# Gated memory attention with an MLP, one core: a tile's outputs gathered through DRAM and summed on VectorE in place of selection matmuls

## The chip, the core and the metric

The kernel runs on one core of a Trainium2 chip. A core has TensorE (matrix multiplication), VectorE, ScalarE, GpSimd, and SyncE, which here only issues DMAs (SP in the profile). The metric is the device time of one execution in microseconds, as the median of several runs.

## The reference, cut to what matters

```python
h = jnp.concatenate([mem, xs], axis=1)          # 8 memory rows and 32 rows of x: one segment of 64
q, k, v = (einsum('btd,dhe->bhte', h, W) for W in (Wq, Wk, Wv))     # 32 heads of 128
scores = where(mask, einsum('bhqe,bhke->bhqk', q, k) * scale, -1e9)
o = einsum('bhqk,bhke->bhqe', softmax(scores), v)
o = einsum('bhte,hed->btd', o, Wo)              # 512 wide
mem = o[:, :8, :]                               # the memory of the next segment
outs.append(o[:, 8:, :])
...
a = concatenate(outs, axis=1)                   # 2048 rows
b = gelu(layernorm(x) @ w1 + b1) @ w2 + b2
out = g * a + (1 - g) * b                       # g = sigmoid(sum(x * gate_w)), one number per row
```

The segments are a recurrence: segment s + 1 needs the 8 memory rows that segment s gives.

## The kernel before, in words

The 2048 rows are 16 tiles (T) of 128 rows; a tile is four segments (si = 0 to 3) of 32 rows. First comes a stage that computes (1 - g) * b for all rows and puts it in DRAM (`c_dr`), while the attention weights are loaded. Then the loop of line 665 runs the 64 segments in order. The order of the instructions on every engine is the order of the program text (`manual_schedule`, line 292); each engine, and SP with its DMAs, takes its own in that order and waits where it must.

A projection or an output projection has 32 columns only, so four matmuls run side by side on four quarters of TensorE's array, each adding up a quarter of the reduction. Such a set of four matmuls of 512 columns is called a unit here. After it the four partial sums of a token lie in four groups of 32 partitions. A segment's main pass has room for 24 of its 32 rows beside the 8 of the memory (`RIDE` = 24); the other 8 rows of each of a tile's four segments (`LEFT` = 8) are collected and done once per tile as extra work, spread in the waits of the recurrence.

One segment of the loop, in the order of the text:

- `prep_h` (GpSimd, line 239) places the next segment's x columns; `x_norm(s-1)` (GpSimd, line 643) scales the previous segment's attention results by the reciprocals of its softmax sums, which come back over DRAM broadcast to all partitions (`Rb`). Its results go into `UT`, for this segment's output projection, and into `UL`.
- SP's loads: in si = 0 `c_load(T-2)` (line 205), `vp_load` (line 182) for the next segment, in si = 0 `load_xT(T+2)` (line 96), a transposing DMA.
- Projections (line 122) into the four banks `U`, each cast by ScalarE (line 127) and transposed by VectorE (line 131); scores; exponentials; the value projection (line 141).
- `run(W1)`: as many pieces of the extra work as W1 says, one unit each. `recip_x` (lines 627 to 635): VectorE's reciprocals, the DMA to `r_dr` (line 630) and back as `Rb` (line 631), the copies into `R`, a copy of the mask (line 252).
- `av`: attention times values (lines 283, 288), and ScalarE's copies into `UT` (line 746).
- `run(W2)`, then the output projection `wo_pass` (line 153) into bank `W`, cast by ScalarE in three cuts into `w` (line 650). `w` holds the four partial sums of the memory rows of this segment and of the other 24 rows of the segment before.
- `run(W3)`, then `out_sel` where there is one.
- `new_mem` in three parts (line 659), with one unit of extra work between them: small matmuls with `SelM` that add the four partial sums of the memory rows, and VectorE's casts into the next `hT` (line 661), from which the next segment's projections read.

The extra work of a tile is dealt out by `side(T, si)`: in si = 0, 1 and 3 projections of the next tile's left rows, eight units each; in si = 2 the output projection of the previous tile's left rows (`wo_left`), whose result `wl` ScalarE casts. Tile 15 has none in si = 0, 1, 3. The numbers of units are in

```python
WS = ((2, 3, 0), (2, 2, 2), (2, 2, 2), (2, 2, 2))
```

`out_sel(T-2)` (lines 221 to 235) is run in si = 0 from T = 2 on, and once for tile 14 behind the loop. It takes the four `w` and the `wl` of tile T - 2 and adds the four partial sums of every row in bank `U[2]`, by four matmuls with the 0/1 matrix `SelR` (line 223) and four with `SelL` (line 227). VectorE then multiplies by g and adds `c` (line 232), and SP stores 128 rows of the output (line 233). That piece is put in VectorE's list `dve_q`, which is emptied at the segment's end.

Of the kernel before, what the change touches and what calls it, by code (L numbers as in the profile page):

```python
# [9 lines left out]
FP32 = mybir.dt.float32  # L10
BF16 = mybir.dt.bfloat16
I32 = mybir.dt.int32
ACTF = mybir.ActivationFunctionType
ALU = mybir.AluOpType
# [13 lines left out]
def kernel(ctx, tc, A_x, A_mem0, A_Wq, A_Wk, A_Wv, A_Wo, A_seg_len, B_x, B_w1, B_b1, B_w2, B_b2, gate_w, out):  # L28
    nc = tc.nc
    P = 128  # L30
    _, S, Dm = A_x.shape
    H, Dh = A_Wq.shape[1], A_Wq.shape[2]
    M = A_mem0.shape[1]
    seg = int(A_seg_len)
# [4 lines left out]
    NT = S // P  # L39
    SPT = P // seg  # L40
# [6 lines left out]
    RIDE = 32 - M  # L47
# [6 lines left out]
    out2 = out.rearrange("b s d -> (b s) d")  # L54

    pers = ctx.enter_context(tc.tile_pool(name="pers", bufs=1))
    dram = ctx.enter_context(tc.tile_pool(name="dram", bufs=1, space=DRAM))
# [4 lines left out]
    ident = pers.tile([P, P], BF16)  # L62
    g_all = pers.tile([P, NT], FP32)
    c_dr = dram.tile([S, Dm], BF16, name="c_dr")
    r_dr = [dram.tile([P, NG], FP32, name=f"r_dr{i}") for i in range(2)]


# [26 lines left out]
    def load_xT(T):  # L94
        xT = ew.tile([P, KC, P], BF16, tag="xT", bufs=3, name="xT")
        nc.sync.dma_start_transpose(out=xT[:], in_=x2[T * P:(T + 1) * P, :])
        xTs[T] = xT
# [7 lines left out]
    U = [lps.tile([P, 512], FP32, name=f"U{i}") for i in range(4)]  # L105
# [55 lines left out]
    def flush(q, n=1):  # L161
        for _ in range(min(n, len(q))):
            q.pop(0)()
# [17 lines left out]
    def vp_load(T, si):  # L181
        nc.sync.dma_start(VP[T % 2][:, si].rearrange("p v e -> p (v e)"), VLs[T][si:P:SPT].rearrange("p a v e -> p a (v e)"))
# [18 lines left out]
    ws, wls, cs = {}, {}, {}  # L201

    def c_load(T):
        c = cw.tile([P, Dm], BF16, tag="c", name="c")
        nc.sync.dma_start(c[:], c_dr[T * P:(T + 1) * P, :])
        cs[T] = c
# [14 lines left out]
    def out_sel(T, bk):  # L221
        for si in range(SPT):
            nc.tensor.matmul(bk[32 * si:32 * si + 32, :], lhsT=SelR[:], rhs=ws.pop(SPT * T + si)[:], start=True, stop=False,
                             skip_group_check=True, tile_position=(0, 32 * si))
        wl = wls.pop(T)
        for si in range(SPT):
            nc.tensor.matmul(bk[32 * si:32 * si + 32, :], lhsT=SelL[:, 32 * si:32 * si + 32], rhs=wl[:], start=False, stop=True,
                             skip_group_check=True, tile_position=(0, 32 * si))

        def ev():  # L230
            o = cw.tile([P, Dm], BF16, tag="o", name="o")
            nc.vector.scalar_tensor_tensor(out=o[:], in0=bk[:], scalar=g_all[:, T:T + 1], in1=cs.pop(T)[:], op0=ALU.mult, op1=ALU.add)
            nc.sync.dma_start(out2[T * P:(T + 1) * P, :], o[:])
        dve_q.append(ev)
        yield

    def prep_h(s):
        T, si = divmod(s, SPT)
        nc.gpsimd.tensor_copy(out=hT[s % 3][:, :, 0:RIDE], in_=xTs[T][:, :, seg * si:seg * si + RIDE])
# [10 lines left out]
    def mask_put(i2):  # L250
        c = 4 * EW + (NG + 2 * M if i2 == 0 else 0)
        nc.vector.tensor_copy(out=(SbF, W)[i2][:, 0:c], in_=MkF[:, 0:c])
# [311 lines left out]
    cw = loop.enter_context(tc.tile_pool(name="cw", bufs=2))  # L564
# [17 lines left out]
    def run(n):  # L582
        for _ in range(n):
            next(fill, None)
# [5 lines left out]
    def side(T, si):  # L590
        gens = []
        if si == 2:
            if T >= 1:
                gens.append(wo_left(T - 1, X1))
        elif T + 1 < NT:
            gens = [[left_qk(T + 1, 0, 0, X1), left_qk(T + 1, 1, 0, X2)], [left_qk(T + 1, 0, 1, X1), left_qk(T + 1, 1, 1, X2)], [],
                    [left_v(T + 1, 0, X1), left_v(T + 1, 1, X2)]][si]
        return chain(*gens)

    def extra(T, si):  # L600

        if si == 0 and T >= 2:
            return out_sel(T - 2, U[2])
        return iter(())

    XRs, Rbs = {}, {}

    xs8 = SbF[:, 4 * EW:4 * EW + NG]
# [29 lines left out]
    def x_norm(s):  # L638
        T, si = divmod(s, SPT)
        XR, Rb = XRs.pop(s), Rbs.pop(s)[:].rearrange("p (c q) (h j) -> p h j c q", c=4, h=2)  # L640
        for out, o, a, b in ((UT[(s + 1) % 2], M, LEFT, 32), (UL[T % 2], LEFT * si, 0, LEFT)):
            for h in range(2):
                nc.gpsimd.tensor_tensor(out=out[:, :, 4 * h:4 * h + 4, o:o + b - a], in0=XR[:, :, 4 * h:4 * h + 4, a:b], in1=Rb[:, h, :, :, a:b], op=ALU.mult)  # L643
# [17 lines left out]
        nc.vector.tensor_copy(out=hn[:, k0:k0 + nk, RIDE:32], in_=bk.rearrange("p (k m) -> p k m", k=nk))  # L661


    WS = ((2, 3, 0), (2, 2, 2), (2, 2, 2), (2, 2, 2))
    for s in range(nseg):
        T, si = divmod(s, SPT)
        last = s == nseg - 1
        hc, hn = hT[s % 3], hT[(s + 1) % 3]
        W1, W2, W3 = WS[si]
        fill = side(T, si)  # L670
        if s + 1 < nseg:
            prep_h(s + 1)
        if s >= 1:
            x_norm(s - 1)
        if si == 0 and T >= 2:
            c_load(T - 2)
        if si < 3:
            vp_load(T, si + 1)
        if last:
            c_load(T - 1)  # L680
            c_load(T)
        if si == 0 and T + 2 < NT:
            load_xT(T + 2)
        for n, (t, hf) in enumerate(((0, 0), (1, 0), (0, 1), (1, 1))):
            bk = U[n]
            for kc in range(KC):
                qk_unit(bk, hc, t, hf, kc)
            if n == 0:
                flush(act_q, 9)
                flush(dve_q, 9)  # L690
            qk_tr(qk_cast(bk[:]), (QT, KT)[t], hf, LEFT * (1 - t))
            if n == 0:
                mask_put(1)
        V = cw.tile([P, NG, Dh], BF16, tag="V", name="V")
        E = cw.tile([P, NG, EW], BF16, tag="E", name="E")
        R = cw.tile([P, NG * 40], FP32, tag="R", name="R")
        Rs[s] = R
        xsum = SbF[:, 0:32 * NG].rearrange("p (i q) -> p i q", q=32)

        def exps(i2, x):  # L700
            c = slice(0, 40) if x else slice(40, EW)
            nc.scalar.activation(out=E[:, 4 * i2:4 * i2 + 4, c], in_=Sb[i2][:, :, c], func=ACTF.Exp, scale=scale)  # L702

        def msum(i2):
            sums(U[i2][:, 320:352].rearrange("p (i q) -> p i q", q=8), E[:, 4 * i2:4 * i2 + 4, :], 40, 48, 8, True)

        def mnorm(i2):
            r, e = RP[i2], E[:, 4 * i2:4 * i2 + 4, 40:56].rearrange("p i (a q) -> p i a q", q=8)
            nc.vector.reciprocal(out=r, in_=U[i2][:, 320:352])
            nc.vector.tensor_tensor(out=e, in0=e, in1=r.rearrange("p (i q) -> p i q", q=8).unsqueeze(2).to_broadcast([P, 4, 2, 8]), op=ALU.mult)  # L710

        scores(s, 0)
        nc.scalar.activation(out=E[:, 0:4, :], in_=Sb[0], func=ACTF.Exp, scale=scale)
        for kc in range(KC):
            v_unit(X1, hc, 0, kc)

        def v_cast(vb, h):
            i0 = 4 * vb + 2 * h
            nc.scalar.copy(out=V[:, i0:i0 + 2, :].rearrange("p i e -> p (i e)"), in_=(X1, X2)[vb][:, 256 * h:256 * h + 256])  # L719

        v_cast(0, 0)
        v_unit(X2, hc, 1, 0)
        if not last:
            xsums(E, 0)
            msum(0)
            mnorm(0)
        scores(s, 1)
        exps(1, 0)
        v_cast(0, 1)
        exps(1, 1)  # L730
        for kc in range(1, KC - 1):
            v_unit(X2, hc, 1, kc)
        if not last:
            msum(1)
            mnorm(1)
        v_unit(X2, hc, 1, KC - 1)
        for h in range(2):
            v_cast(1, h)
        if last:
            break  # L740
        run(W1)
        xsums(E, 1)
        recip_x(s)
        av(s, V, E)
        for j in (0, 2, 1, 3):
            nc.scalar.copy(out=UT[s % 2][:, j, :, 0:M], in_=U[j][:, 0:NG * 40].rearrange("p (i q) -> p i q", q=40)[:, :, 32:40])  # L746
        x_raw(s)
        run(W2)
        prep_q(s + 1)
        w = wo_pass(UT[s % 2], (0, P, 2 * P, Dm))  # L750
        if s >= 1:
            ws[s - 1] = w
        run(W3)
        for _ in extra(T, si):
            pass
        new_mem(w, hn, 0)
        run(1)
        new_mem(w, hn, 1)
        run(1)
        new_mem(w, hn, 2)  # L760
        for _ in fill:
            pass
        if si == 3 and T + 2 < NT:
            left_x(T + 2)
        flush(dve_q, 9)
        nc.vector.tensor_tensor(out=rmin[:, 0:RW], in0=rmin[:, 0:RW], in1=R[:, 0:RW], op=ALU.min)
        flush(act_q, 9)
# [33 lines left out]
    wl, c = wls.pop(T), cs.pop(T)  # L801
# [11 lines left out]
    o = cw.tile([P, Dm], BF16, tag="o", name="o")  # L813
# [128 lines left out]
```

## Time and profile before

| | |
|---|---|
| median of 3 runs | 770.96 us (770.31 to 771.15) |
| span of the profiled execution, first to last instruction | 768.4 us |
| mean granted TensorE clock in it | 0.996 |
| busy: TensorE, ScalarE, VectorE, GpSimd | 753.4, 540.0, 396.1, 278.2 us |
| 16 DMA engines, queue of SP | 26.8% of their time |

The profiled execution's time is known by its span; what lies around it (start and end of the program) is the 2.6 us to the median. Times in rows are microseconds from the span's start. A row of a merged view has start, length, engine, line, what is written and read, how many instructions; a bracket at its end tells how long the engine was idle before it and what ended that. In rows of groups the numbers behind the bar are the busy time in all, the mean of one in ns, and the idle time before them. PEld is TensorE's loading of weights, which lies beside its matmuls. Rows with SPq are SP's DMA issues: the length is that of the issue, not of the transfer.

### The profile page before, as it was taken

How to read it: one execution, taken by the hardware profiler on the slowest of the kernel's cores; microseconds unless marked ns; L12 is line 12 of the kernel's file. 1: busy time of each engine (PE TensorE's matmuls, PEld its weight loads, DVE VectorE, ACT ScalarE, POOL GpSimd, SP SyncE). 2: the span in 40 equal slices, each digit the busy share in tenths (PEclk: the TensorE clock that was granted, in tenths of full speed). 3: DMA queues.
4: the chain of work that ended last, by engine and by line, in shares of the span. 5: the costliest groups of instructions: out<-in, count | busy, mean ns of one | idle time of the engine just before them, and what ended most of it. 6: DMA issues, size and time to landing. Idle time of an engine off the chain costs nothing.

```text
span 768.4 us, 43822 instructions
## 1 busy us (share of the span) xinstructions
PE 753.4 (98%) x19186; PEld 412.2 (54%) x19186; DVE 396.1 (52%) x1428; ACT 540.0 (70%) x1631; POOL 278.2 (36%) x522
## 2 busy tenths in 40 slices
PE   7999999999999999999999999999999999999996
PEld 5666554555555555555555555555555555555553
DVE  5776355445445454545554554545454555444444
ACT  4666676777777777777777777777777777777763
POOL 4111033433344443334434334443424443343341
PEclk9999999999999999999999999999999999999999
DMA  6779422223222222212131322122222213122221
GB/s 196 274 233 400 153 58 63 76 63 87 65 59 66 79 72 73 80 53 74 58 89 62 90 63 79 45 80 73 80 72 59 76 49 89 62 83 64 72 67 38
DMA packets 53319, 70.58 MB, mean 92 GB/s; under 512 B 21306, under 2 KB 43043, under 8 KB 51587
## 3 DMA queue, kind: packets, MB, share of 16 engines
q1 hardware_dynamic: 51394, 64.84, 26.8%
q8 instruction: 152, 2.49, 1.4%
q0 software_dynamic: 784, 1.97, 0.8%
q10 hardware_dynamic: 944, 0.92, 0.3%
q14 instruction: 45, 0.36, 0.2%
HBM read 56.96 MB, written 4.45 MB: 80 GB/s over the span
## 4 chain that ended last, share of the span: by engine, by line
PE 96%; DMA 1%; DVE 1%; ACT 1%; issue 0%; SPq 0%; POOL 0%; DVEq 0%; ACTq 0%
PE U L122 30%; PE X L141 18%; PE W L153 15%; PE X L122 7%; PE U L468 4%; PE U L283 4%; PE X L153 4%; PE W L462 2%; PE SbF L462 2%; PE U L270 1%; PE W L259 1%; DMA w_sb<-in_B_w_dram 1%; PE U L659 1%; PE SbF L259 1%; PE SbF L616 1%; PE U L288 1%
## 5 line engine op out<-in xcount | busy, mean ns | idle before, releaser
L643 POOL TENSOR_TENSOR UT<-XR,Rb 128x384 bf16<-128x384 bf16 x126 | 140.3, 1136 | 301.7 <-DMA Rb<-r_dr 220.5
L127 ACT CAST Tb<-U 128x512 bf16<-128x512 f32 x258 | 151.2, 586 | 78.4 <-PE U L122 78.1
L122 PEld LDWEIGHTS <-hT 128*32 128x32 bf16 x4096 | 104.5, 96 | 103.9 <-DVE hT L661 8.6
L141 PE MATMUL X<-Wv_sb,hT 128*32 128x512 bf16 x2048 | 143.8, 378 | 0.0
L122 PE MATMUL U<-Wq_sb,hT 128*32 128x512 bf16 x2048 | 136.1, 381 | 0.3 <-DVE hT L661 0.2
L122 PE MATMUL U<-Wk_sb,hT 128*32 128x512 bf16 x2048 | 132.7, 379 | 0.0
L153 PE MATMUL W<-Wo_sb,UT 128*32 128x512 bf16 x2080 | 124.6, 380 | 1.2 <-POOL racc L635 1.2
L661 DVE CAST hT<-U 128x8 bf16<-128x8 f32 x126 | 20.9, 167 | 172.8 <-PE U L659 163.6
L719 ACT CAST V<-X 128x256 bf16<-128x256 f32 x256 | 88.7, 372 | 14.5 <-PE X L141 0.8
L131 DVE STREAM_TRANSPOSE QT<-Tb 128x256 f32<-128x256 f32 x128 | 57.0, 446 | 76.5 <-ACT Tb L127 76.5
L153 PEld LDWEIGHTS <-UT 128*32 128x32 bf16 x2080 | 57.8, 96 | 56.5 <-issue 13.1
L650 ACT CAST w<-W 128x128 bf16<-128x128 f32 (+1 forms) x192 | 46.0, 311 | 48.2 <-PE W L153 48.2
L622 ACT CAST XR<-U 128x256 bf16<-128x256 f32 x252 | 78.4, 434 | 0.0
L131 DVE STREAM_TRANSPOSE KT<-Tb 128x256 f32<-128x256 f32 x128 | 57.0, 445 | 28.0 <-ACT Tb L127 23.5
L643 POOL TENSOR_TENSOR UL<-XR,Rb 128x128 bf16<-128x128 bf16 x126 | 60.3, 502 | 0.0
L141 PEld LDWEIGHTS <-hT 128*32 128x32 bf16 x2048 | 46.4, 94 | 21.0
L635 POOL TENSOR_TENSOR racc<-racc,R 128x72 f32<-128x72 f32 x63 | 21.3, 338 | 93.4 <-PE U L288 84.1
L468 PE MATMUL U<-w_sb,hTm 128*128 128x512 bf16 (+1 forms) x176 | 52.4, 381 | 0.0
L746 ACT CAST UT<-U 128x64 bf16<-128x64 f32 x252 | 35.4, 226 | 22.9 <-PE U L288 22.8
L462 PEld LDWEIGHTS <-w_sb 128*128 128x128 bf16 (+1 forms) x352 | 34.5, 102 | 20.1 <-issue 1.3
L702 ACT ACTIVATE E<-W 128x64 bf16<-128x64 f32 (+1 forms) x128 | 35.0, 273 | 11.3 <-PE W L263 11.3
L659 PEld LDWEIGHTS <-w 128*32 128x32 bf16 x1008 | 22.8, 93 | 37.2 <-ACT w L650 29.3
(159 smaller groups left out, 1204.7 us busy)
## 6 DMA issues: line engine op xcount, KB each, us to landing
Rb<-r_dr SPq DMA_DIRECT2D x63, 512.0 KB, 3.8
Wv_sb<-in_A_Wv_dram SPq DMA_DIRECT2D x4, 1024.0 KB, 6.3
Wq_sb<-in_A_Wq_dram SPq DMA_DIRECT2D x4, 1024.0 KB, 7.1
Wk_sb<-in_A_Wk_dram SPq DMA_DIRECT2D x4, 1024.0 KB, 9.4
Wo_sb<-in_A_Wo_dram SPq DMA_DIRECT2D x4, 1024.0 KB, 15.0
VP<-VL SPq DMA_DIRECT2D x64, 64.0 KB, 3.5
c<-c_dr SPq DMA_DIRECT2D x16, 128.0 KB, 3.6
xt<-in_A_x_dram SPq DMA_DIRECT2D x15, 128.0 KB, 3.1
```

Of the source, the lines that this page charges most:

```text
L122: nc.tensor.matmul(bk[32 * j:32 * j + 32, :], lhsT=G[:, kc, :], rhs=W5[t][:, kc, h0:h1, j, :], start=(kc == 0), stop=(kc == KC - 1), tile_ ...
L127: nc.scalar.copy(out=Tb[:], in_=bk.rearrange("p (a b e) -> p a e b", a=8, b=2))
L131: nc.vector.transpose(out=dst[:, 8 * hf:8 * hf + 8, c0:c0 + 32, :].rearrange("p a r b -> p a (r b)").bitcast(FP32), in_=Tb[:].rearrange("p ...
L141: nc.tensor.matmul(bk[32 * j:32 * j + 32, :], lhsT=G[:, kc, :], rhs=Wv5[:, kc, 4 * vb:4 * vb + 4, j, :], start=(kc == 0), stop=(kc == KC - ...
L153: nc.tensor.matmul(bk[32 * c:32 * c + 32, :], lhsT=U_[:, j, i, :], rhs=Wo_sb[:, 4 * i + j, :], start=(n == 0), stop=(n == NW - 1), tile_po ...
L462: nc.tensor.matmul(hp[:rows, 0:TB * P], lhsT=w1_sb[:, kc, fc * P:fc * P + rows], rhs=yTs[blk][:, kc, :], start=(kc == 0), stop=(kc == KC - 1))
L468: nc.tensor.matmul(bp(blk, tt)[:], lhsT=hTm[blk % 2][:rows, fc, tt * P:(tt + 1) * P], rhs=w2_sb[:rows, fc, :], start=(fc == 0), stop=(fc = ...
L622: nc.scalar.copy(out=XR[:, j], in_=U[j][:, 0:NG * 40].rearrange("p (i q) -> p i q", q=40)[:, :, 0:32])
L643: nc.gpsimd.tensor_tensor(out=out[:, :, 4 * h:4 * h + 4, o:o + b - a], in0=XR[:, :, 4 * h:4 * h + 4, a:b], in1=Rb[:, h, :, :, a:b], op=ALU ...
L650: nc.scalar.copy(out=w[:, a:b], in_=W[:, a:b])
L719: nc.scalar.copy(out=V[:, i0:i0 + 2, :].rearrange("p i e -> p (i e)"), in_=(X1, X2)[vb][:, 256 * h:256 * h + 256])
L746: nc.scalar.copy(out=UT[s % 2][:, j, :, 0:M], in_=U[j][:, 0:NG * 40].rearrange("p (i q) -> p i q", q=40)[:, :, 32:40])
```

## The change

Outputs of tiles 0 to 13 no longer go through `out_sel` in the loop. Instead:

- `put_w`: each segment's `w` (128 x 512, four partial sums) is stored to DRAM at the top of the segment two later.
- `get_w`: two segments after that, the 24 rows are loaded back, so that the four partial sums of a token lie side by side in one partition of a tile `G` (128 x 4 x 512).
- `put_left`: `wl` of tile T - 1 is stored at the top of si = 3 of tile T; `get_left(T-2)`: at the top of si = 0 of tile T four DMAs load the 8 rows per segment of tile T - 2 from there into `G`.
- `add_parts(T-2)`: three additions and the multiply-add with g and `c` on VectorE, two of the four in si = 0 and two in si = 1 of tile T, placed behind `x_raw`; then the store of the output.
- W1, W2, W3 become 2, 2, 2 in every segment. `out_sel` stays for tile 14, behind the loop, and the last tile's own end is as it was.

All the new DMAs are issued by SP. The `w_dr` and `l_dr` buffers are double, by the parity of the tile.

```diff
+    w_dr = [dram.tile([SPT, P, Dm], BF16, name=f"w_dr{i}") for i in range(2)]
+    l_dr = [dram.tile([P, Dm], BF16, name=f"l_dr{i}") for i in range(2)]
...
+    def put_w(s, w):
+        T, si = divmod(s, SPT)
+        nc.sync.dma_start(w_dr[T % 2][si], w[:])
+
+    def put_left(T):
+        nc.sync.dma_start(l_dr[T % 2][:], wls.pop(T)[:])
+
+    def get_w(s):
+        T, si = divmod(s, SPT)
+        if si == 0:
+            Gs[T] = cw.tile([P, 4, Dm], BF16, tag="G", name="G")
+        nc.sync.dma_start(Gs[T][seg * si:seg * si + RIDE], w_dr[T % 2][si].rearrange("(c r) e -> r c e", c=4)[M:32])
+
+    def get_left(T):
+        for si in range(SPT):
+            nc.sync.dma_start(Gs[T][seg * si + RIDE:seg * si + seg],
+                              l_dr[T % 2][:].rearrange("(c i m) e -> i m c e", c=4, i=SPT)[si])
+
+    def add_parts(T):
+        a, G = cw.tile([P, Dm], FP32, tag="acc", bufs=1, name="acc"), Gs.pop(T)
+        nc.vector.tensor_tensor(out=a[:], in0=G[:, 0], in1=G[:, 1], op=ALU.add)
+        yield
+        nc.vector.tensor_tensor(out=a[:], in0=a[:], in1=G[:, 2], op=ALU.add)
+        yield
+        nc.vector.tensor_tensor(out=a[:], in0=a[:], in1=G[:, 3], op=ALU.add)
+        yield
+        o = cw.tile([P, Dm], BF16, tag="o", name="o")
+        nc.vector.scalar_tensor_tensor(out=o[:], in0=a[:], scalar=g_all[:, T:T + 1], in1=cs.pop(T)[:], op0=ALU.mult, op1=ALU.add)
+        nc.sync.dma_start(out2[T * P:(T + 1) * P, :], o[:])
         yield
...
-    def extra(T, si):
-
-        if si == 0 and T >= 2:
-            return out_sel(T - 2, U[2])
-        return iter(())
-
...
-    WS = ((2, 3, 0), (2, 2, 2), (2, 2, 2), (2, 2, 2))
+    adds = iter(())
...
-        W1, W2, W3 = WS[si]
...
         if si == 0 and T + 2 < NT:
             load_xT(T + 2)
+        if s >= 2 and s - 2 < SPT * (NT - 2):
+            put_w(s - 2, ws.pop(s - 2))
+        if 4 <= s < SPT * (NT - 2) + 4:
+            get_w(s - 4)
+        if si == 3 and 1 <= T < NT - 1:
+            put_left(T - 1)
+        if si == 0 and T >= 2:
+            get_left(T - 2)
+            adds = add_parts(T - 2)
...
-        run(W1)
+        run(2)
         xsums(E, 1)
         recip_x(s)
         av(s, V, E)
...
         x_raw(s)
-        run(W2)
+        for _ in range(2):
+            next(adds, None)
+        run(2)
         prep_q(s + 1)
         w = wo_pass(UT[s % 2], (0, P, 2 * P, Dm))
         if s >= 1:
             ws[s - 1] = w
-        run(W3)
-        for _ in extra(T, si):
-            pass
+        run(2)
         new_mem(w, hn, 0)
```

More of the change, by code (lines that the diff above doesn't have):

```diff
@@ L234, in out_sel @@
         dve_q.append(ev)
+        yield
+    Gs, accs = {}, {}
+    def put_w(s, w):
[19 more added lines that the diff above has]
+        nc.vector.tensor_tensor(out=a[:], in0=a[:], in1=G[:, 3], op=ALU.add)
+        yield
+        o = cw.tile([P, Dm], BF16, tag="o", name="o")
+        nc.vector.scalar_tensor_tensor(out=o[:], in0=a[:], scalar=g_all[:, T:T + 1], in1=cs.pop(T)[:], op0=ALU.mult, op1=ALU.add)
+        nc.sync.dma_start(out2[T * P:(T + 1) * P, :], o[:])
         yield
```

## The prediction, as it was made

> **What bounds the kernel now.** I read the page first: its span, and the chain of work that ended last by engine.
>
> ```profile
> span 768.4 us, 43822 instructions
> PE 96%; DMA 1%; DVE 1%; ACT 1%; issue 0%; SPq 0%; POOL 0%; DVEq 0%; ACTq 0%
> ```
>
> The chain lies almost wholly on TensorE. Taken alone that says: whatever leaves TensorE shortens the kernel. So I went on to the chain in order of time, where each segment begins with one merged row of 64 projection matmuls (line 122). The distance of two such starts is the length of a segment. Here are tile 1 (four segments), the first two segments of tile 7, and the first of tile 15.
>
> ```profile
> 137.35 3.55 PE U L122 x64
> 148.01 3.45 PE U L122 x64
> 158.14 3.55 PE U L122 x64
> 168.37 3.55 PE U L122 x64
> 178.60 3.55 PE U L122 x64
> ...
> 385.93 3.55 PE U L122 x64
> 396.58 3.48 PE U L122 x64
> 406.74 3.55 PE U L122 x64
> ...
> 718.00 3.55 PE U L122 x64
> 728.19 3.51 PE U L122 x64
> ```
>
> Tile 1: 10.66, 10.13, 10.23, 10.23 us. Tile 7: 10.65, then 10.16. Three things are to be seen. The first segment of a tile is about 0.42 us longer than an ordinary one. Tile 1 has no selection matmuls yet (they start at T = 2) and its first segment is as long as that of tile 7, which has them. And tile 15 runs its first segment without any fill (there is no tile 16 to prepare) in 10.19 us: the eight fill units of four matmuls each stand in waits that exist anyway. What bounds a segment is the recurrence (projections, scores, softmax, values, output projection, new memory), not the amount of matmuls. Then the chain inside the first segment of tile 7:
>
> ```profile
> 392.79 0.76 PE X L122 x12
> ...
> 395.28 0.22 PE U L223 x4
> 395.50 0.22 PE U L227 x4
> ...
> 396.35 0.23 PE X L122 x4
> ```
>
> The selection matmuls take 0.44 us in the place in which TensorE must wait for the first cast of `w` in any case. What makes the segment long is WS = (2, 3, 0): a third fill unit in front of the output projection (the row with x12, where other segments have x8), and so a last unit left behind the new memory (the row at 396.35). These are 0.22 us each.
>
> **What the change takes away.** With runs of 2, 2, 2 in every segment, the first segment becomes like the third: 10.23 us. The second now begins without its small lead: 10.23 for 10.13. For tile 1 the four sum to 41.25 us before and 4 x 10.23 = 40.92 after, 0.33 us less; tiles 0 to 14 give 15 x 0.33 = 4.9 us. Tile 15 has no fill and gives nothing. With 112 selection matmuls fewer (14 tiles of 8) TensorE loses work, but I give that no further credit, because the two fill units that take the place cover the same wait. VectorE also loses one evacuation (line 232) per tile at the segment's boundary, where no chain row names it: nothing.
>
> **What the change adds on VectorE.** Per tile three additions of 128x512 and one multiply-add from SBUF, two in segment si = 0 and two in si = 1, behind the mask copy (line 252) and ahead of the new memory's casts (line 661), which are on the chain. The nearest row with this shape from SBUF is the gate's multiply-add; the last row below is a cast that ends the idle stretch.
>
> ```profile
> L447 DVE SCALAR_TENSOR_TENSOR junk<-xt,gw_bc 128x512 bf16<-128x512 bf16 x16 | 11.0, 687 | 0.3
> ```
>
> ```profile
> 392.78 0.42 DVE L252 CAST SbF<-MkF 128x248 f32<-128x248 bf16 x1
> ```
>
> ```profile
> 403.37 0.42 DVE L252 CAST SbF<-MkF 128x248 f32<-128x248 bf16 x1
> 406.35 0.44 DVE L661 CAST hT<-U 128x8 bf16<-128x8 f32 x2 [2.56 <-PE U L659]
> ```
>
> Two operations are 1.37 us (bounds: 1.37 by this row, 1.5 by the old evacuation from PSUM at 0.75 each). In si = 1 of tile 7 VectorE is idle from 403.79 to 406.35: 1.37 fit, nothing is lost. In si = 0 it is idle from 393.20. The cast is due there at 9.77 + 0.07 = 9.84 us after the segment's start (9.77 is 406.35 - 396.58; 0.07 the lead that only si = 1 has), so at 395.77. The two casts after it leave about 0.07 us. So the additions must begin by 395.84 - 1.37 - 0.05 for the wake-up = **394.42**, or the whole recurrence waits. Their cover is 1.2 us if the data are there at 393.20. They are not.
>
> **What it adds on SP.** This is where the sum is decided. The data of the additions come last from `get_left(T-2)`, four DMAs issued at the top of the same segment, behind everything that SP has there. SP's own timeline for tile 7:
>
> ```profile
> 386.62 0.53 SPq L182 DMA_DIRECT2D VP<-VL  x1
> 387.20 0.58 SPq L205 DMA_DIRECT2D c<-c_dr  x1
> 387.84 0.73 SPq L182 DMA_DIRECT2D VP<-VL  x1
> 388.62 1.28 SPq L96 DMA_TRANSPOSE xT<-in_A_x_dram  x1
> 392.62 0.33 SPq L630 DMA_DIRECT2D r_dr<-R  x1
> ...
> 397.39 0.34 SPq L233 DMA_DIRECT2D out_dram<-o  x1
> 397.77 0.55 SPq L182 DMA_DIRECT2D VP<-VL  x1
> ```
>
> SP is busy without a gap until 389.90, then free until `r_dr`. Behind 389.90 + 0.04 come `put_w` (as the store of `out`, 0.38 from start to start: 390.32), `get_w` (as the load of `c`, 0.64: 390.96) and the four `get_left`. A load of few partitions is seen once in the prologue, and how long a landing takes is in the lines for `r_dr` (4 KB, the first line of the second fence) and `c` (128 KB, its second):
>
> ```profile
> 51.37 0.48 SPq L348 DMA_DIRECT2D m<-in_A_mem_dram  x1
> 51.89 2.13 SPq L314 DMA_DIRECT2D Wq_sb<-in_A_Wq_dram  x2
> ```
>
> ```profile
> DMA to landing us min/median/max: 1.4/1.5/3.3
> ```
>
> ```profile
> DMA to landing us min/median/max: 2.3/3.6/4.4
> ```
>
> The 8 rows of `m0` go out at 0.52 from start to start; with one wait more on SP for its semaphore I take 0.58 (VP to `c` above; bounds 0.38 and 0.64). So the fourth starts at 390.96 + 3 x 0.58 = 392.70. It moves 32 KB; between the quickest landings, 1.4 for 4 KB and 2.3 for 128 KB, a straight line gives 1.6, and I take 1.7 (bounds 1.4 and 3.6). Landing: **394.40, against a deadline of 394.42**. The tile of the example is just in time, with no reserve.
>
> Other tiles are not. The transposing load, whose issue is in the path, takes longer in some:
>
> ```profile
> L96 SPq DMA_TRANSPOSE xT<-in_A_x_dram x16: 1242/1302/2611, 48.7 to 637.6; - x16
> ```
>
> ```profile
> 181.09 1.58 SPq L96 DMA_TRANSPOSE xT<-in_A_x_dram  x1
> ```
>
> ```profile
> 637.59 2.08 SPq L96 DMA_TRANSPOSE xT<-in_A_x_dram  x1
> ```
>
> Of the twelve tiles that have both (T = 2, the first, to T = 13, the last) the issue ends later than in tile 7, counted from the segment's start, by 0.10, 0.52, 0.68, 0.71, 0.28 (T = 2 to 6), 0.92 and 0.61 (T = 12, 13), and 0.2 earlier in T = 8 to 11: together 3.8 us of lateness, or 3.7 with the 0.02 of reserve taken off each. `r_dr` lands 1.9 us behind its minimum at worst; for such disturbed landings among the last of the four I add an estimated 0.15 per tile, 1.8 us. T = 14 has no transposing load and T = 15 neither; they pay nothing. While VectorE waits for the data, the new memory's casts are queued behind it, and TensorE waits for those: each late microsecond counts in full.
>
> A rule of the Trainium skill speaks against the landing that I take. The page "DMA: Bandwidth & Descriptors", section "Anatomy of one DMA", gives a fixed part of about 2.0 us per DMA (fitted on another issuing path) plus bytes over 436 GB/s, about 2.1 us for 32 KB. That is above the 1.4 that `r_dr` shows here and below the 3.6 of `c`; by it the four would land 0.4 us later and the forecast would be about 4 to 5 us higher, an estimate.
>
> **What else is moved.** `r_dr` of that segment now goes out when SP is done, at about 393.3 instead of 392.62, so `Rb` lands up to 0.7 us later and GpSimd normalises later in the next segment. The nearest case without much room:
>
> ```profile
> 452.09 2.23 POOL L643 TENSOR_TENSOR UT<-XR,Rb 128x384 bf16<-128x384 bf16 x2 [6.15 <-DMA Rb<-r_dr]
> ```
>
> ```profile
> 455.25 1.91 PE L153 MATMUL W<-Wo_sb,UT 128*32 128x512 bf16 x32
> ```
>
> Even here the part that TensorE needs is done at 454.32, 0.93 us early, so the 0.7 is covered: nothing; without the cover at most 12 x 0.7 = 8 us. In the other segments `put_w` and `get_w` go out once `w` is cast, near the segment's end, behind `Rb` in the same queue and long before the next `r_dr`: nothing. `put_left` goes out a whole segment before it is read. Bound below nothing: fewer matmuls may leave TensorE's instruction stream less disturbed, which no row prices.
>
> **Sum.** -4.9 + 3.7 + 1.8 = +0.6 on the profiled execution. The span of 768.4 lies 2.6 us under the median of 770.96, which is taken as unchanged around it: 771.6 us.
>
> **The rivals.**
> *All hidden.* The four go out at the store's 0.38 and land in 1.5: 390.96 + 1.14 + 1.5 = 393.6, 0.8 us early. Then only the latest two or three tiles pay, some 0.5 us together: 770.96 - 4.9 + 0.5 = 766.5. For it: 128 partitions of `out` go out in 0.34. Against it: `m0` with 8 rows takes 0.48.
> *Late in every tile (slower).* It decides at one place: VectorE at the first addition of si = 0. If the fourth lands as `c` at its quickest, 2.3 us, each of twelve tiles pays 0.6 on top, some 7 us: 778.5; at the median of 3.6, 1.9 each, 22 us: 794. It decides from a landing of 1.75 us on. For it: `c`, issued in the same stretch, has that median. Against it: `c` is four times the size and stands behind a larger load.
> *TensorE's work counts after all.* If the 0.44 us of selection were on the path in 14 tiles, 6.2 us would go with them and no wait came: 764.8. Tile 1 speaks against it.
>
> **How the numbers follow.** Forecast (late by tenths in some tiles, 768 to 776): 0.45. All hidden: 0.30. Late in every tile: 0.20. TensorE's work: 0.05. No change means within 0.2%, about 1.5 us, which is what a measurement of this kernel can tell apart. The forecast's case holds both signs: 0.02 faster, 0.18 same, 0.25 slower. So faster 0.37, same 0.18, slower 0.45. The range 766 to 784 leaves out the credit for TensorE, a part of the hidden case, and the landing like the median of `c`; the forecast's own range is 768 to 776.
>
> **What would show it.** Right: the first segments with selection gone are 10.2 us where the data are in time, tiles 0 and 1 for certain; SP issues six DMAs in a row behind the transposing load; VectorE's first addition in si = 0 is idle before it until a DMA of G, and the new memory's cast comes later by as much; tiles 14 and 15 do not wait. Wrong: the addition starts right behind the mask copy everywhere (all hidden), or GpSimd's normalisation becomes what the output projection waits for, or the second segment of a tile grows by more than 0.1 us.

## The result and the profile after

The changed kernel takes **781.37 us** (median of four runs, 779.98 to 785.22) against 770.63 us for the kernel before beside it: ratio 1.0150, interval 1.0123 to 1.0177. It is 10.7 us slower. The forecast was 771.6 us; its rival "late in every tile" gave 778.5 us for a landing of 2.3 us and 794 us for one of 3.6 us.

Each run gives two numbers, its time and the span of its instructions. The span is the better measure of what goes on inside the kernel, because the time around it isn't the same for all kernels (last section): 1.8 us for the kernel before in the runs made beside these experiments, 2.3 us for the changed one. (The 2.6 us named ahead of the prediction are the distance from the profiled execution to the median of other runs, so part of them is the spread of the runs.) By spans the change costs 779.1 (median of 777.8, 778.1, 780.1 and 782.9) - 768.8 (770.63 less 1.8) = 10.3 us. The profiled execution is the slowest of the four, so sums over its rows come out some 4 us too high. A span also holds the stage ahead of the loop, which all these kernels share and which does not always take equally long; where that matters it is said.

From the page of the changed kernel, the span and the chain that ended last by engine:

```profile
span 782.9 us, 43891 instructions
PE 88%; DMA 3%; ACT 2%; DVE 2%; SPq 2%; issue 2%; POOL 1%; DVEq 0%; ACTq 0%; POOLq 0%
```

Before, TensorE held 96% of the chain. Now it holds 88%, and the rest has gone to DMAs, SP's queue and what waits for them. The chain in order of time, with the starts of the projections (row: start, length): the first two segments of tile 1, the first two of tile 7, the first of tile 14.

```profile
137.00 3.55 PE U L124 x64
147.24 3.55 PE U L124 x64
...
389.28 3.55 PE U L124 x64
...
401.09 3.64 PE U L124 x64
411.41 3.55 PE U L124 x64
...
689.97 3.55 PE U L124 x64
700.20 3.55 PE U L124 x64
```

Tile 1 (no output to collect yet): 10.24 us, where it was 10.66. Tile 14 (no transposing load): 10.23. The forecast 10.23 is there in both. Tile 7: 11.81 by these rows. From start to start of the first query projections the first segments of tiles 2 to 13 take 11.01 to 12.56 us (tile 7 11.97), together 14.3 us above twelve times 10.23. SP's issues in that segment of tile 7 show the queue behind the transposing load:

```profile
391.77 1.29 SPq L98 DMA_TRANSPOSE xT<-in_A_x_dram  x1
393.10 0.99 SPq L243 DMA_DIRECT2D w_dr<-w  x1
394.14 0.40 SPq L252 DMA_DIRECT2D G<-w_dr  x1
394.58 1.76 SPq L256 DMA_DIRECT2D G<-l_dr  x4
396.45 0.34 SPq L659 DMA_DIRECT2D r_dr<-R  x1
```

The four left loads have left SP at 396.34, 7.06 us after 389.28. VectorE over the same stretch, from the mask copy to the new memory's cast:

```profile
396.46 0.42 DVE L287 CAST SbF<-MkF 128x248 f32<-128x248 bf16 x1
399.55 0.69 DVE L261 TENSOR_TENSOR acc<-G 128x512 f32<-128x512 bf16 x1 [2.67 <-DMA G<-l_dr]
400.27 0.69 DVE L263 TENSOR_TENSOR acc<-acc,G 128x512 f32<-128x512 f32 x1
400.88 0.23 DVE L690 CAST hT<-U 128x8 bf16<-128x8 f32 x2
```

VectorE is ready at 396.88 and stands idle for 2.67 us until the left rows are in. The two additions then run, and the cast on which the next projections hang starts at 400.88, 11.60 us into the segment; without a wait it was due at about 9.84. The waits of the whole kernel (engine, line, who ended it: us in all, times, longest) say the same, with one trap:

```profile
PE U L124 <- DVE hT L690: 11.8, 12, 2.1
DVE acc L261 <- DMA r_dr<-R: 23.5, 10, 3.5
DVE acc L261 <- DMA G<-l_dr: 6.4, 3, 2.7
```

TensorE's projections wait 11.8 us for the cast, twelve times: once for each of tiles 2 to 13. VectorE's wait before the first addition is put down ten times to `r_dr`, the DMA issued right behind the left loads, and three times to the left loads. But an addition reads nothing of `r_dr`, and experiment `e2_left_first` shows it starting before the `r_dr` DMA has even left SP. A wait for several semaphores is named after the one that came last by the profile, and both land within a tenth or two of each other.

### The profile page after: what moved, and what is told of

It is laid out like the page before. It is cut to its first block, busy times and chain, and to the rows that moved or that the text cites. A ratio compares the mean times of both kernels' runs of the same rounds, so it can differ in the third digit from the quotient of the medians.

```text
span 782.9 us, 43891 instructions
## 1 busy us (share of the span) xinstructions
PE 754.3 (96%) x19074; PEld 410.5 (52%) x19074; DVE 425.3 (54%) x1470; ACT 538.6 (69%) x1631; POOL 291.5 (37%) x522
## 4 chain that ended last, share of the span: by engine, by line
PE 88%; DMA 3%; ACT 2%; DVE 2%; SPq 2%; issue 2%; POOL 1%; DVEq 0%; ACTq 0%; POOLq 0%
PE U L124 28%; PE X L143 17%; PE W L155 14%; PE X L124 6%; PE U L503 5%; PE U L318 4%; PE X L155 3%; PE W L497 2%; PE SbF L497 2%; PE U L305 1%; PE W L294 1%; DMA r_dr<-R 1%; PE U L688 1%; ACT w L679 1%; PE SbF L294 1%
## 5 line engine op out<-in xcount | busy, mean ns | idle before, releaser
L124 PE MATMUL U<-Wq_sb,hT 128*32 128x512 bf16 x2048 | 137.2, 383 | 11.8 <-DVE hT L690 11.8
L155 PE MATMUL W<-Wo_sb,UT 128*32 128x512 bf16 x2080 | 126.9, 384 | 1.7 <-POOL racc L664 1.2
```

The costliest lines, as they stand in the source:

```text
L124: nc.tensor.matmul(bk[32 * j:32 * j + 32, :], lhsT=G[:, kc, :], rhs=W5[t][:, kc, h0:h1, j, :], start=(kc == 0), stop=(kc == KC - 1), tile_ ...
L155: nc.tensor.matmul(bk[32 * c:32 * c + 32, :], lhsT=U_[:, j, i, :], rhs=Wo_sb[:, 4 * i + j, :], start=(n == 0), stop=(n == NW - 1), tile_po ...
```

## The experiments

All ran in five rounds beside the kernel before. The table gives the median time, the ratio with its interval, and the median span less that of before in the same rounds. Where outputs are left out, the expectation says which.

| run | time us | ratio (interval) | span, difference |
|---|---|---|---|
| `e4_no_sel_222` | 767.68 | 0.9955 (0.9942 to 0.9968) | -4.9 |
| `e12_stores_only` | 769.45 | 0.9983 (0.9970 to 0.9995) | -2.55 |
| `e6_dmas_only` | 769.79 | 0.9984 (0.9969 to 1.0000) | -0.85 |
| `e1_adds_later` | 770.57 | 1.0001 (0.9989 to 1.0012) | -0.1 |
| the change | 781.37 | 1.0150 (1.0123 to 1.0177) | +10.3 |
| `e2_left_first` | 771.89 | 1.0018 (1.0003 to 1.0032) | +0.65 |
| `e7_one_load` | 774.43 | 1.0052 (1.0033 to 1.0070) | +4.35 |
| `e3_no_sel` | 772.62 | 1.0039 (1.0026 to 1.0053) | +0.4 |
| `e5_sel_222` | 769.66 | 0.9995 (0.9983 to 1.0008) | -0.8 |
| `e8_traffic_twice` | 773.36 | 1.0030 (1.0012 to 1.0048) | +3.2 |
| `e9_sbuf_direct` | 775.60 | 1.0087 (1.0059 to 1.0115) | +5.45 |
| `e11_left_si1` | 770.43 | 1.0009 (0.9992 to 1.0026) | -0.2 |
| `e10_direct_left_si1` | 768.61 | 0.9976 (0.9965 to 0.9987) | -1.85 |

Several runs came out beside every value that was expected of them: `e1_adds_later` and `e2_left_first` some 4 us above the 766 to 768 of the theory below, `e6_dmas_only` between its two, `e4_no_sel_222` 2 us in time above its 765.7, `e7_one_load`, `e5_sel_222` and `e8_traffic_twice` just outside theirs, `e9_sbuf_direct` above both of its own. The first three lead to what the DMAs cost, further down.

The theory was that the additions in si = 0 wait for the landing of the left loads. The rivals were that the new traffic itself costs the time, that VectorE's added work does, or that SP's longer queue delays something else.

### Only the place of the additions: `e1_adds_later`

```diff
         if si == 0 and T >= 2:
             get_left(T - 2)
+        if si == 1 and T >= 2:
             adds = add_parts(T - 2)
```

> The additions of a tile are placed one segment later (si = 1 and 2 in place of 0 and 1); every DMA stays where it is. Theory A (the loss is VectorE's wait for the last load of left rows, which holds back the new memory's casts): no first segment waits any more, all are 10.2 us, and the whole gain of the even runs is left: 766, about 4.9 under the kernel before. Theory B (the loss is the added DMA traffic itself: later broadcasts, instruction fetches, landings): the traffic is the same, so it stays at 778 to 782. Theory C (the additions' own time on VectorE): the loss moves to another segment and stays at 778 to 782.

Measured: 770.57 us, 10.8 below the change, with every DMA and every addition kept. Tile 7's first two segments by the chain:

```profile
385.56 3.54 PE U L124 x64
395.79 3.55 PE U L124 x64
406.02 3.55 PE U L124 x64
```

Both are 10.23. VectorE in the second one starts the addition right behind the mask copy, and the cast that follows is not pushed (its wait is for TensorE):

```profile
402.65 0.42 DVE L287 CAST SbF<-MkF 128x248 f32<-128x248 bf16 x1
402.98 0.81 DVE L261 TENSOR_TENSOR acc<-G 128x512 f32<-128x512 bf16 x1
403.82 0.71 DVE L263 TENSOR_TENSOR acc<-acc,G 128x512 f32<-128x512 f32 x1
405.63 0.44 DVE L690 CAST hT<-U 128x8 bf16<-128x8 f32 x2 [1.11 <-PE U L688]
```

So the loss is the wait in si = 0, not VectorE's work and not SP's queue.

### Only the place of the loads: `e2_left_first`

```diff
+        if si == 0 and T >= 2:
+            get_left(T - 2)
         if si == 0 and T + 2 < NT:
             load_xT(T + 2)
...
         if si == 0 and T >= 2:
-            get_left(T - 2)
             adds = add_parts(T - 2)
```

> The four loads of left rows go ahead of the transposing load on SP, the additions stay in si = 0 and 1. Theory A: the last of the four is issued about 3 us earlier, at 4.0 us of the segment, and lands at 6.8 even with the 2.7 us that it took; the deadline is 8.5: 766 to 768. Theory B: same traffic, 778 to 782. If the transposing load in front made the landing long, the landing falls to about 1.7 us.

Measured: 771.89 us. SP in tile 7, then VectorE:

```profile
388.23 1.55 SPq L256 DMA_DIRECT2D G<-l_dr  x4
...
392.78 0.99 SPq L659 DMA_DIRECT2D r_dr<-R  x1
```

```profile
392.84 0.42 DVE L287 CAST SbF<-MkF 128x248 f32<-128x248 bf16 x1
393.17 0.68 DVE L261 TENSOR_TENSOR acc<-G 128x512 f32<-128x512 bf16 x1
```

The left loads are issued about 3 us earlier in the segment, and the wait is gone (in tile 13 the addition still waits 1.2 us, but starts in time). The addition starts at 393.17 while the issue of `r_dr` lasts to 393.77: it does not wait for `r_dr`. The landing itself did not get shorter. By the trace's semaphore counts the fourth left load of tiles 2 to 13 lands 2.58 to 3.80 us after the start of its issue (median 2.72); in the changed kernel it is 2.25 to 3.39 (median 2.62). So neither the transposing load just ahead nor the place in the queue is what made it long.

### One load for four: `e7_one_load`

```diff
+        nc.sync.dma_start(Gs[T][RIDE * si:RIDE * si + RIDE], w_dr[T % 2][si].rearrange("(c r) e -> r c e", c=4)[M:32])
...
     def get_left(T):
-        for si in range(SPT):
-            nc.sync.dma_start(Gs[T][seg * si + RIDE:seg * si + seg],
-                              l_dr[T % 2][:].rearrange("(c i m) e -> i m c e", c=4, i=SPT)[si])
+        nc.sync.dma_start(Gs[T][RIDE * SPT:P], l_dr[T % 2][:].rearrange("(c q) e -> q c e", c=4))
```

> The changed kernel with the tile G in another order of rows, so that the left rows come in one load of 32 partitions in place of four of 8 (the rows of the outputs of tiles 0 to 13 are mixed up within their tile). The additions stay in si = 0. If the landing of 2.7 us is that of any load from DRAM here, the load goes out at about 5.8 us of the segment and lands at 8.4, the deadline being 8.5: most of the 10.8 us that the additions' place cost are back, 770 to 773. If a load of 8 partitions is slow by its shape, the landing falls under 2 us as well: 770 to 771. If four issues on SP or the landing did not matter: 779 to 782.

Measured: 774.43 us, between the change and `e2_left_first`. The single load goes out some 1.2 us earlier than the fourth of four did, and that is what is won; it lands later after its issue (2.49 to 4.20 us in tiles 2 to 13, median 3.15, for four times the bytes). VectorE still waits:

```profile
DVE acc L259 <- DMA G<-l_dr: 20.4, 12, 2.7
```

Fewer DMAs help by the issue time they save, not by a quicker landing.

### The gain by itself: `e4_no_sel_222`, `e3_no_sel`, `e5_sel_222`

All three start from the kernel before. `e3_no_sel` drops `out_sel` in the loop and keeps WS, `e5_sel_222` keeps `out_sel` and makes WS even, `e4_no_sel_222` does both:

```diff
-        if si == 0 and T >= 2:
-            return out_sel(T - 2, U[2])
         return iter(())
...
-    WS = ((2, 3, 0), (2, 2, 2), (2, 2, 2), (2, 2, 2))
+    WS = ((2, 2, 2), (2, 2, 2), (2, 2, 2), (2, 2, 2))
```

> The kernel before with runs 2, 2, 2 and without the selection matmuls, so the outputs of tiles 0 to 13 are left out: all that the change takes away and nothing that it adds. My account of the gain: 15 tiles by 0.33 us, 765.7. If the selection matmuls counted by TensorE's time: 764 or less.

> The kernel before with its runs 2, 3, 0 and without the selection matmuls, so the outputs of tiles 0 to 13 are left out. Theory of the prediction (the matmuls stand in a wait that is there anyway, the long first segment comes from the order of the fill): first segments stay at 10.6 us and the time within 1 us of 770.7. Rival (they count by TensorE's time, 0.44 us in 14 tiles): 764.5 to 765.5.

> The kernel before with runs 2, 2, 2 in si = 0 and its selection matmuls kept behind them, no other change. By the prediction's account a unit in place costs 0.22 us when no wait is left for it: two more units behind the third run give 14 x 0.44 = 6.2 on the 4.9 less of the even runs, so 770 to 773. If the selection matmuls were free in any place: 766.

Measured: `e4_no_sel_222` has 764.0 us of span against 768.9, so -4.9 us, the forecast's own term; in time it is -3.0 because 3.7 us instead of 1.8 lie around its span. `e3_no_sel`: +0.4 by the span, nothing gained; its 772.62 us of time has the same 3.7 around it. `e5_sel_222`: -0.8. The projections' starts show the arrangement. Tile 1, then tile 7's first and second segment, of `e3_no_sel`:

```profile
137.85 3.55 PE U L122 x63
148.51 3.45 PE U L122 x64
...
386.29 3.55 PE U L122 x63
...
397.24 3.45 PE U L122 x64
407.38 3.55 PE U L122 x64
```

Tile 1's first segment is 10.66 and tile 7's 10.95 then 10.14, with no selection matmul in the loop. The median of the first segments of tiles 1 to 14 is 10.64 here and in the kernel before: under (2, 3, 0) the selection matmuls cost nothing. The same for `e4_no_sel_222`, tile 1:

```profile
136.68 3.55 PE U L122 x64
146.91 3.55 PE U L122 x64
157.14 3.55 PE U L122 x64
```

10.23 and 10.23. In `e5_sel_222` the first segments of tiles with selection are 10.56 (median, start to start), 0.33 longer than without. So under even runs the selection matmuls are on the path, with somewhat less than the 0.44 that the expectation took. The 4.9 us need both edits together; either alone gives under one, which is about what these runs can tell apart.

### What the DMAs cost: `e6_dmas_only`, `e12_stores_only`, `e8_traffic_twice`

`e6_dmas_only` is the change without the additions and the output stores behind them, `e12_stores_only` that without the loads back, `e8_traffic_twice` is `e6_dmas_only` with a second store of each `w` and a second gather, from DRAM to DRAM:

```diff
         if si == 0 and T >= 2:
             get_left(T - 2)
-            adds = add_parts(T - 2)
```

```diff
-        if 4 <= s < SPT * (NT - 2) + 4:
-            get_w(s - 4)
...
-        if si == 0 and T >= 2:
-            get_left(T - 2)
```

```diff
         nc.sync.dma_start(w_dr[T % 2][si], w[:])
+        nc.sync.dma_start(w2_dr[T % 2][si], w[:])
...
+        nc.sync.dma_start(w3_dr[SPT * (T % 2) + si][:], w2_dr[T % 2][si].rearrange("(c r) e -> r c e", c=4)[M:32])
```

> The changed kernel with all its new DMAs but without the additions and the stores, so the outputs of tiles 0 to 13 are left out. Theory A: nothing waits for the loads, 766. Theory B: 775 to 782, as the traffic is all there but for the stores.

> The kernel with the DMAs but without additions, and here without the loads back (get_w, get_left) as well: only the stores put_w and put_left are left. The outputs of tiles 0 to 13 are missing. By the spans, the kernel without any of these DMAs stood 4.9 us below the kernel before, and the one with all of them 0.9 us below it, so the DMAs cost 4.0 us. Theory S, the stores do it (8.8 MB written, read from w while TensorE reads it, ahead of Rb in no case): the span stands 0.5 to 1.5 us below that of before. Theory L, the loads do it (their issues and their landings among VP and Rb): the span stands 4 to 5 us below. Theory B, both in proportion to their bytes (8.8 and 7.2 MB): about 2.7 us below. Ratio of times 0.998 to 1.000 under S, 0.994 to 0.996 under L, 0.9965 under B, if the time around the span stays at 1.8 us.

> The kernel with the new DMAs only (no additions), with a second store of w and a second gather of its rows, from DRAM to DRAM, in every segment: the traffic of the rows is doubled, nothing waits for it. Theory: the 2.1 us between the kernel without selection and the one with the DMAs are TensorE's stops for want of instructions, which come later the more the DMA engines carry: about 2 us more, 771 to 773, and the waits of TensorE's weight loads for issue rise from 47.6 to 53 us or more. Rival (the 2.1 us are a matter of SP's order, or chance): 769 to 770.5 and the same waits.

Measured by spans: -4.9 with no new DMA, -2.55 with the stores, -0.85 with stores and loads, +3.2 with the traffic doubled. In these first three no operation uses new data, and yet the DMAs cost 4.05 us. By the spans alone theory B of `e12_stores_only` would hold, 2.35 for the stores and 1.7 for the loads. By the times, of which 3.6 to 3.7 us lie around the first two spans, the three stand at 767.68, 769.45 and 769.79. Where the time goes is better seen in the profiled executions; those of `e4_no_sel_222` and `e12_stores_only` are each within 0.3 us of their kernel's median span. The first and the last segment by their chains, in this order:

```profile
95.82 3.57 PE U L122 x64
...
744.76 3.55 PE U L122 x64
```

```profile
97.16 3.57 PE U L124 x64
...
746.24 3.55 PE U L124 x64
```

From the first segment to the last they take 648.94 and 649.08 us. The difference of the two spans, 1.8 us, lies for 1.34 ahead of the loop, in code that both share and before any of the new stores; it is there already when the first load of one of the attention's weights, `Wv_sb`, goes out, at 19.20 and at 20.54 us. `e6_dmas_only` takes 653.42 for the same stretch, and its profiled execution is 1.4 above its kernel's median. So in the loop the stores cost nothing that these profiles show, and some 3 us come with the loads back, which is theory L and not B, by one profile of each kernel.

Part of it can be seen; why it happens cannot. TensorE's weight loads ahead of the output projection stop for no event that the profile shows; three kernels, in this order the kernel before, `e4_no_sel_222` and `e6_dmas_only`:

```profile
PEld L153 <- issue: 13.2, 43, 0.3
```

```profile
PEld L153 <- issue: 17.7, 55, 0.6
```

```profile
PEld L155 <- issue: 19.5, 57, 0.8
```

Most of these lie beside running matmuls, but some do not. An example of `e6_dmas_only`, in the third segment of tile 7, which is 10.91 us long:

```profile
417.33 0.61 PE L155 MATMUL X<-Wo_sb,UL 128*32 128x512 bf16 x6 [0.32 <-issue]
```

From the 5th segment to the 60th TensorE is idle in such stops (those over 0.1 us) for 0.3 us before, 1.5 in `e4_no_sel_222`, 0.9 in `e12_stores_only`, 3.3 in `e6_dmas_only` and 4.0 in `e1_adds_later`, one profile each: here too it is the loads that bring more. In `e8_traffic_twice` they do not grow (2.9); there the loss is another, GpSimd's normalisation late behind `Rb`:

```profile
PEld L157 <- POOL UT L676: 8.2, 10, 1.4
```

So that more traffic lengthens the stops is not shown; why the loads cost time stays open.

### Without DRAM: `e9_sbuf_direct`, and a mended pair: `e10_direct_left_si1`, `e11_left_si1`

`e9_sbuf_direct` is `e1_adds_later` with `put_w` and `get_w` replaced by four copies from `w` to `G` in SBUF:

```diff
-        nc.sync.dma_start(w_dr[T % 2][si], w[:])
+        for c in range(4):
+            nc.sync.dma_start(Gs[T][seg * si:seg * si + RIDE, c], w[32 * c + M:32 * c + 32])
```

> A version meant to be better: additions in si = 1 and 2, and the 24 rows of a segment copied straight from w to G within SBUF by four DMAs of 24 rows, two segments later than the store was, no way through DRAM for them: 96 KB moved per segment in place of 224. If the traffic by bytes is what costs the 2.1 us: 768.5 to 769.5, under the kernel before. If the number of DMAs on SP counts: 770 to 772.

Measured: 775.60 us, slower. SP in the first two segments of tile 10:

```profile
515.50 4.12 SPq L245 DMA_DIRECT2D G<-w  x4
519.66 1.49 SPq L252 DMA_DIRECT2D G<-l_dr  x4
521.26 0.35 SPq L655 DMA_DIRECT2D r_dr<-R  x1
523.80 0.34 SPq L656 DMA_DIRECT2D Rb<-r_dr  x1
```

These four copies take 4.12 us, the longest such group of the run; the median of the groups is 3.07, or 0.77 for a copy of 24 rows inside SBUF. Four of them and the four left loads stand ahead of `r_dr`, and its way back as `Rb`; GpSimd's normalisation is then late for the second segment's output projection, which is the cover that the prediction put at "at most 12 x 0.7" when gone:

```profile
PEld L154 <- POOL UT L668: 9.8, 15, 1.4
```

So the left loads were moved to si = 1, where SP has room: in this kernel (`e10_direct_left_si1`) and in the one over DRAM (`e11_left_si1`, from `e1_adds_later`):

```diff
-        if si == 0 and T >= 2:
+        if si == 1 and T >= 2:
             get_left(T - 2)
             adds = add_parts(T - 2)
```

> The direct copies within SBUF, with the four loads of left rows moved from the top of si = 0 to the top of si = 1, ahead of the additions in si = 1 and 2. In the run with direct copies GpSimd waited 4.7 us of TensorE's time for the broadcast in si = 1, since SP was still issuing copies when the sums of si = 0 were ready. If SP's queue in si = 0 is what cost that: those waits go and the time is 768 to 770. If the copies themselves cost: it stays at 774 to 776.

> The kernel with the additions in si = 1 and 2, and the loads of left rows also moved to the top of si = 1; the rows of w go over DRAM as in the change. It shortens SP's queue in si = 0 and changes no traffic. If the queue in si = 0 costs something there: 768 to 769.5. If it is the traffic: 770 to 771 as before the move.

Measured: 768.61 us for the first, 0.9976 (0.9965 to 0.9987) of the kernel before: faster than both kernels, by 1.9 and 12.8 us. GpSimd's lateness is almost gone:

```profile
PEld L154 <- POOL UT L668: 0.9, 3, 0.3
```

The second is 770.43, no different from `e1_adds_later`: over DRAM, SP's queue in si = 0 cost nothing. The two kernels differ in the way of the 24 rows alone, and 1.65 us of span lie between them: part of what the new DMAs cost goes with the way through DRAM, which also moves more bytes.

## Why the prediction was right or wrong

By spans the runs give a sum to set beside the prediction's own: -4.9 (`e4_no_sel_222`), +4.05 (the new DMAs, `e6_dmas_only`), +0.75 (the additions in si = 1 and 2 and the output stores, `e1_adds_later`), +10.4 (their place in si = 0). Each term is the difference of two runs that stand next to each other, so they must add up to the measured +10.3; 0.5 us more lies around the span.

- **"15 x 0.33 gives 4.9 us": right**, -4.9 by the median spans (the spread of the runs leaves some half a microsecond). In the profiled executions an undisturbed tile falls from 41.25 to 40.92 us, as forecast; the loop as a whole gives 3.5 (652.33 to 648.86 from the first to the last query projections), as more stops come in. The reading behind it, that a first segment is as long without selection as with it, holds as well (`e3_no_sel`).
- **"I give that no further credit" for the selection matmuls: right in the sum.** They are free in the old arrangement and worth 0.33 per tile in the new one, so they had to go for the even runs to pay.
- **The deadline of the first addition: right within 0.2 us.** It was set 8.49 us into the segment; the runs put it at about 8.68. In tile 14 the addition starts at 8.69 and the segment takes 10.24; in each of the tiles 2 to 13 the segment grows by the start of the addition less 8.68, to a few hundredths.
- **The issue of the fourth load, 6.77 us into the segment of tile 7: right**, at 6.91. The parts were off and made up for each other: the loads go out 0.35 apart where no issue is held up, not 0.58, while `put_w` and sometimes a left load keep SP longer (0.99 for `put_w` in tile 7, where 0.38 was taken). Tile by tile the lateness was not the one read from the kernel before: tile 12, put 0.92 later, came at 6.77, and tile 8, put 0.2 earlier, at 8.48, because the load ahead of its fourth kept SP for 1.45 us. In sum over the twelve tiles it was 2.8 us late; the term for it was 3.7.
- **"I take 1.7" for the landing: this is the step that failed.** It was 2.25 to 3.39 us, median 2.62. The straight line between `r_dr` (1.4 us, 4 KB) and `c` (2.3 us, 128 KB) mixed a store to DRAM with a load from it, and went by size alone. The row of the same kind was `c`: its quickest landing was 2.3, and of the twelve left loads on which an addition waited one came in under that. With a landing 0.92 longer the terms 3.7 + 1.8 become 13.8 + 1.8 (tiles 8 to 11, taken as 0.2 early, pay that much less), and the prediction's own working gives 781.7. The first segments of the profiled execution, the slowest, show 14.3, the median spans 10.4. That the measured 781.4 is so near 781.7 is luck: the place of the additions cost less, and a cost of the DMAs that was put at nothing, below, makes up for it.
- **The rival "late in every tile"** named the mechanism, the place and the price; it "decides from a landing of 1.75 us on", and every one of the twelve was past that. What was held against it, that `c` is "four times the size", is worth little by `e7_one_load`: four times the bytes took half a microsecond more.
- **The Trainium skill** ("DMA: Bandwidth & Descriptors", section "Anatomy of one DMA", a fixed 2.0 us, by which 32 KB are an estimated 2.1) was nearer than the line between rows. The traces agree that the fixed part dominates (2.62 us for 32 KB, 3.15 for 128 KB in `e7_one_load`), and put the whole half a microsecond above the estimate.
- **"In the other segments ... nothing"** for the DMAs: wrong by about 4 us by the spans and some 3 by the loops of the profiled executions, in scattered segments and without a wait that the profile can name. The prediction's line that fewer matmuls "may leave TensorE's instruction stream less disturbed" saw that such a term can exist, but not its sign: such stops became more.
- **`r_dr` moved later is covered: right**, for the changed kernel; `e9_sbuf_direct` shows the cover gone once 3 to 4 us of copies stand ahead of it.
- **"T = 15 ... pay nothing": wrong in the profiled execution**, whose first segment of tile 15 takes 12.61 us. Its additions wait for nothing there; the clock fell (next section).

## What to carry to other kernels

For a small load from DRAM, take the quickest landing of the nearest load from DRAM as the least to expect, whatever its size, and not a line drawn through a store. When an operation is queued ahead of a recurrence's own cast on the same engine, its data must land early enough for the operation to end within that engine's slack; if they cannot, move the operation to the next segment before thinking about the transfer. Here that took back 10.4 us, and left the change level with the kernel before: the gain of 4.9 us went to the DMAs and the additions. Two edits can be worth 4.9 us together and under one each, so test the pair. And before a difference of two spans is put down to an edit, see in which stage it lies: of the 1.8 us between two of the profiled executions here, 1.3 lay ahead of the loop that the edit is in.

## What the runs showed of the hardware

**The granted clock fell once after a wait of about 2 us.** TensorE's first row after the wait at the start of tile 8's second segment, then windows of the changed kernel around it (us, busy time of PE, PEld, DVE, ACT and POOL, granted clock, share of the DMA engines, GB/s):

```profile
444.28 1.05 PE L124 MATMUL U<-Wq_sb,hT 128*32 128x512 bf16 x16 [2.12 <-DVE hT L690]
```

```profile
441.89:445.30 3.41, 1.29 (x33) 0.76 (x32) 2.54 (x9) 0.94 (x2) 0.00 (x0) 1.00 0.38 146
445.31:448.71 3.40, 3.40 (x40) 1.37 (x32) 1.28 (x4) 1.17 (x2) 1.48 (x2) 0.50 0.33 102
```

TensorE stood for 2.12 us. In the 3.41 us ahead of 445.30 it was busy for 1.29; for the next 3.40 the granted clock was 0.50, and that segment's projections took 5.32 us in place of 3.55. Of the twelve waits this is the longest and the only one with such an aftermath. The Trainium skill ("TensorE: Matmul & The Clock Gate", section "What's actually happening") has the clock at half after an idle window of about 3.4 us; the half agrees with the trace, but here a wait of 2.12 was enough. In tile 15's first segment, which has neither fill nor selection, the clock fell as well:

```profile
738.90:742.50 3.60, 3.54 (x32) 1.23 (x32) 1.34 (x2) 1.32 (x6) 1.50 (x2) 0.53 0.47 152
```

Why it fell there stays open. The 3.40 us ahead of it (735.44 to 738.84) hold 2.37 us of TensorE's work, and the 3.41 from 397.53 hold 2.30 without a fall behind them. The same segment took 10.21 us in the kernel before, with the selection matmuls in it, and 10.2 to 10.8 in the experiments, most of which leave them out too; so their absence alone does not bring it. Both falls belong to this one execution: its mean granted clock is 0.991, that of the other three of the changed kernel 0.996 to 1.000, and two such falls take 0.004 off.

**The time around the span differs from kernel to kernel.** It is 1.8 us (within 0.1) in every run of the kernel before and of seven of the experiments, 1.9 in `e11_left_si1`, 2.3 in the change and `e2_left_first`, and 3.6 to 3.7 in `e3_no_sel`, `e4_no_sel_222` and `e12_stores_only`. What makes it was not tried.

**SP's issue time does not follow the bytes.** In the changed kernel a left load (8 rows of four pieces, 32 KB) takes 0.30 us in the median, the load of 24 rows (96 KB) 0.40; the copy of 24 rows inside SBUF in `e9_sbuf_direct` (24 KB) took 0.72.
